# Moving row scatters off the products' ends, one block's scores ahead of the fourth turn, and the first tile's transposes into the fifth turn

## The chip, the cores and the metric

The kernel runs on one core of a Trainium2 chip. The metric is the time of one execution on the device in microseconds (us). The core has five engines with queues of their own: PE (TensorE, matrix products and transposes), DVE (VectorE), ACT (ScalarE), POOL (GpSimd) and SP (SyncE, which here issues DMAs). PSUM is the memory that PE writes its results to; SBUF holds everything else on the chip.

## The reference

Two steps: a linear attention with decay over 4 batches, 8 heads and 768 positions, worked through block by block with a running state, and a mixture of experts that sends each of the 3072 resulting rows (512 values) to one of 8 experts.

```
# attention, for each block of rows (the reference uses 64, the kernel 128)
intra = (qb @ kb.T) * Dmask;  intra = intra @ vb
inter = (qb * lam_pow) @ kv_state
out[:, :, sl] = intra + inter
kv_state = lam_block * kv_state + (kb * rev_pow).T @ vb

# experts, x = the attention's rows
logits = x @ w_gate + modality_bias[modality_id]
e_idx = argmax(logits);  gate_w = probability of that expert
h = maximum(x[mask] @ w1[e], 0)
out[mask] = gate_w[mask] * (h @ w2[e])
```

## The kernel before

**The attention** goes over 24 blocks of 128 rows, numbered 0 to 23, six to a batch. A loop over m (lines 926 to 991) takes the pair a = 2m, b = 2m+1. For each block PE makes the scores (`scores`, L261, tile `s` in two PSUM buffers), DVE multiplies them by the decay mask (`mask`, L267, tile `pt`), ACT scales the keys (`keys`, L243, tile `kd`) and POOL the queries (`query`, L228, tile `qd`); then PE multiplies the queries by the state (`from_state`, L309), the masked scores by the values (`values`, L319), and the keys by the values (`products`, L275, tile `kv`), and DVE adds these products to the state (`add`, L283 and L286). Scores, masks, keys and queries are made one pair ahead. Results gather in the tile `o`, which has two buffers, and are copied to `xt` (`give`, L298), the last block's on DVE.

**Turns.** After each second pair, four blocks (a group, 0 to 5) are turned from columns to rows: `turns(grp, amid)` calls `turn` for two blocks (PE transposes L338, copied on DVE L345 and ACT L348 to the tile `grp`), then `gates` (PE, L356), and then `turn` for two more. The last group comes later, within the first products of the experts. The third group stands in m = 5, the fourth in m = 7, the fifth in m = 9.

**Routing.** For each third of the rows (8 blocks) DVE chooses experts and slots. The many small DVE instructions are a list from which `do(n)` takes the next n (they show up as L384). Then eight scatters (`one_slot`, L439) write rows to `placed`, a tensor in the chip's main memory, in the order of their experts: a short POOL copy (L442) and an indirect DMA that POOL issues (L443). They wait in the list `jobs`, and `tick(mm)` takes the next one and ties its DMA to a PE instruction `mm`. The eight scatters of the first third are called 0 to 7 here; they enter the list after the third group's turn in m = 5, and all must be issued by m = 8, where `need("slots")` empties the list and the first tile of rows is fetched.

**The first tile of the experts.** `fetch_x(0)` (L616, SP) reads 512 rows back from `placed` into `xg` with four DMAs; it waits for the landing of the last scatter. `turn_rows(0)` transposes them on DVE in two halves (L690), `split_rows` makes a rounded part and a rest of them (ACT and DVE, tile `xhl`), and `low_w1` and `split` make the rest `low` of the weights (DVE, L915 and L611). All of that feeds the first layer (L702 to L704), of which PE does a first part ahead of the last group's turn. From there on PE works through the experts' tiles.

**The order.** PE, DVE, ACT and SP run their instructions in the order in which the code issues them. POOL's are chained in theirs by `pool()`. Nothing is reordered by a scheduler; a tick adds a wait and does not place anything on PE.

Of the kernel before, what the change touches and what calls it, by code (L numbers as in the profile page):

```python
# [15 lines left out]
P = 128  # L16
# [27 lines left out]
def linear_attention_moe(tc, qkv, lam, modality, wg, mbias, w1, w2, out):  # L44
    nc = tc.nc
    with ExitStack() as ctx:
# [199 lines left out]
        scs = {}  # L246
# [9 lines left out]
        def scores(g):  # L256
            kt, qt, vt, kn = loaded(g)
            scs[g] = ps.tile([P, 2, NP, P], F32, name="s", bufs=2)
            for p in range(NP):
                for hl, r in enumerate(halves2):  # L260
                    mm = nc.tensor.matmul(scs[g][:, hl, p, :], kt[r, p, :], qt[r, p, :], start=True, stop=True)  # L261
            begun[g] = mm
            return mm
# [93 lines left out]
                                          start=(p == 0), stop=(p == NP - 1), tile_position=(0, t * Q))  # L357
            return mm

        def turns(grp, amid):  # L360
            turn(grp, 0)
            turn(grp, 1)
            mm = gates(grp)
            do(4)
            amid()
            turn(grp, 2)
            return mm, turn(grp, 3)

        shape = [P, RC, E]

# [317 lines left out]
        def turned(out, rows):  # L688

            return nc.vector.transpose(out=out.rearrange("q p (t a) -> q t p a", a=Q),  # L690
                                       in_=rows.rearrange("q t (p a) -> q t p a", a=Q))

        def turn_rows(n):
            for h in range(2):
                turned(xt2[:, :, h * P : (h + 1) * P], xgs[n][:, 4 * h : 4 * (h + 1), :])

        def split_rows():
            for i in range(2):
# [126 lines left out]
        xgs = {}  # L825
# [30 lines left out]

        pairs = B * NC // HB
        def block(g, on_pool=False):
            mm = scores(g)
            mask(g)  # L860
            keys(g, on_pool)
            query(g)
            return mm
# [62 lines left out]
        for m in range(2, pairs):  # L926
            a, b = HB * m, HB * m + 1
            ahead = m + 1 < pairs
            add(b)
            if m == 4 or m == 8:  # L930
                routed = m // 4 - 1, *choose(m // 4 - 1, gate_rows())
            if ahead:
                block(a + 2)
                mm = block(b + 2)
                if m > 4:
                    tick(mm)
                if 2 < m <= pairs - SLOTS:
                    after(load(m + SLOTS - 1, [1]), mm)
                if m == 9:
                    fetch_w1(*some, parts=range(2, 4))  # L940
                elif m == 10:
                    fetch_w2(*some, parts=range(2, 4))
            if m == 5 or m == 9:
                ranks(routed[-1])
                slots += slots_of(*routed)
            if m == 10:
                w1h = w1_part("w1h", F32R, True)
                w1l0 = [work.tile([P, KC, TT], F32R, name="low", tag=f"both{i}" if i < 4 else "dk", bufs=1) for i in range(1, 5)]
                nc.scalar.copy(out=w1h[0], in_=raw1[0])
                do(4)  # L950
                turn_rows(0)
            elif not ahead:
                split_rows()
                low_w1(0)
                split(raw1[1], w1h[1], w1l0[1])
                do(4)
            elif m == 2:
                routing_constants()
            elif m == 3:
                clear(slice(E * CAP, E * CAP + TT), TT)  # L960
            if m < 10:
                do(7 if m % 4 == 0 else 8)
            if m == 2:
                mm = values(b, begins=True)
                from_state((a, b), ends=True)
            elif not ahead:
                values(a, begins=True)
                mm = values(b, begins=True)
                from_state((a, b), ends=True)
            else:  # L970
                from_state((a, b))
                values(a)
                mm = values(b)
            if m == 4 or m == 8:
                do(1)
            if m > 4:
                tick(mm)
            if m + SLOTS < pairs:
                load(m + SLOTS, [0])
            if ahead:  # L980
                mm = products(a + 2)
                mm = products(b + 2) or mm
                if m == 7:
                    tick(mm)
                add(a + 2)
            if m % 2 and ahead:
                ends = turns(m // 2, begin_list)
                if m == 5 or m == 9:
                    jobs += [("slots", one_slot)] * RC
                for mm in ends[: 2 if m % 4 == 1 else 1] if m > 4 else ():  # L990
                    tick(mm)
            if m == 8:
                need("slots")
                raw1 = w1_part("raw1", F32)
                some = fetch_regs(0, True)
                fetch_w1(*some, parts=range(2))
                fetch_x(0)
            elif m == 9:
                raw2 = w2_part("raw2", F32)
                some = fetch_regs(0, True)  # L1000
                fetch_w2(*some, parts=range(2))
                fetch_x(1)
# [195 lines left out]
```

## Time and profile before

| what | us |
|---|---|
| median of 3 runs | 383.61 (383.05 to 384.69) |
| the profiled execution | 384.85 |
| its span | 383.1 |
| PE busy | 373.5 |
| DVE busy | 282.9 |
| ACT busy | 237.4 |
| POOL busy | 99.0 |

The span is what the trace covers, from the first instruction to the last. A timeline gives for each stretch of like instructions its start, its duration from the first start to the last end, the engine and line, the tile written and those read, their shapes and the number of instructions. Idle time of the engine just before it, when there is any that counts, stands at the end in brackets with what ended it. The end of a matrix product in the record is modelled and reaches into the next one's start by about 0.07 us. A POOL row of an indirect DMA is the time that POOL takes to write its descriptors, not the transfer.

### The profile page before, as it was taken

How to read it: one execution, taken by the hardware profiler on the slowest of the kernel's cores; microseconds unless marked ns; L12 is line 12 of the kernel's file. 1: busy time of each engine (PE TensorE's matmuls, PEld its weight loads, DVE VectorE, ACT ScalarE, POOL GpSimd, SP SyncE). 2: the span in 40 equal slices, each digit the busy share in tenths (PEclk: the TensorE clock that was granted, in tenths of full speed). 3: DMA queues.
4: the chain of work that ended last, by engine and by line, in shares of the span. 5: the costliest groups of instructions: out<-in, count | busy, mean ns of one | idle time of the engine just before them, and what ended most of it. 6: DMA issues, size and time to landing. Idle time of an engine off the chain costs nothing.

```text
span 383.1 us, 9168 instructions
## 1 busy us (share of the span) xinstructions
PE 373.5 (97%) x3316; PEld 318.1 (83%) x3316; DVE 282.9 (74%) x506; ACT 237.4 (62%) x458; POOL 99.0 (26%) x130
## 2 busy tenths in 40 slices
PE   8999999999999999999999999999999999999993
PEld 3889989888998889888888877788878888888882
DVE  6677978779777889867789584486876868688630
ACT  1577676777766765564766664456566665776621
POOL 3653238628600177020100102102011020201112
PEclk9999999999999999999999999999999999999998
DMA  7999988999979684599714899763870210300100
GB/s 246 386 408 385 363 315 282 394 294 354 295 255 292 230 232 180 220 347 326 208 52 122 268 409 313 285 191 91 290 233 30 56 55 19 93 0 3 55 29 27
DMA packets 44597, 82.69 MB, mean 216 GB/s; under 512 B 7406, under 2 KB 20222, under 8 KB 44544
## 3 DMA queue, kind: packets, MB, share of 16 engines
q1 hardware_dynamic: 40592, 69.23, 55.6%
q0 software_dynamic: 3952, 12.79, 8.8%
q8 instruction: 28, 0.46, 0.5%
q14 instruction: 25, 0.20, 0.2%
HBM read 89.52 MB, written 17.85 MB: 280 GB/s over the span
## 4 chain that ended last, share of the span: by engine, by line
PE 56%; issue 33%; POOL 5%; DVE 3%; DMA 2%; SPq 0%; POOLq 0%; ACT 0%; DVEq 0%
PE s L742 8%; PE o L702 6%; PE o L704 6%; PE o L703 6%; PE s L261 6%; PE o L319 5%; POOL out_dram L770 4%; PE o L338 3%; PE s L741 3%; PE o L309 3%; PE kv L275 2%; DMA load<-in_qkv_dram 2%; PE x L356 1%; PE s L704 1%; PE kv L702 1%
## 5 line engine op out<-in xcount | busy, mean ns | idle before, releaser
L742 PE MATMUL s<-xhl,w1h 128*128 128x512 f32 x320 | 108.2, 395 | 0.0
L770 POOL DMA_INDIRECT out_dram<-y,idx x24 | 28.7, 1198 | 213.1 <-ACT y L769 167.8
L702 PE MATMUL o<-w2h,hh 128*128 128x512 f32 x192 | 75.1, 391 | 0.0
L703 PE MATMUL o<-w2l,hh 128*128 128x512 f32 x192 | 74.8, 389 | 0.0
L704 PE MATMUL o<-w2h,hl 128*128 128x512 f32 x192 | 74.7, 389 | 0.0
L741 PE MATMUL s<-xhl,w1l 128*128 128x256 f32 x240 | 67.2, 280 | 0.0
L742 PEld LDWEIGHTS s<-xhl,w1h 128*128 128x128 f32 x320 | 55.2, 188 | 7.7 <-issue 0.4
L751 DVE TENSOR_TENSOR hs<-s,hb 128x512 f32<-128x512 f32 x40 | 27.6, 690 | 43.8 <-ACT hb L749 43.8
L611 DVE TENSOR_TENSOR w1l<-raw,w1h 128x1024 fp32r<-128x1024 f32 x44 | 51.7, 1220 | 2.0 <-ACT w1h L610 2.0
L753 DVE TENSOR_TENSOR w2l<-raw,w2h 128x1024 fp32r<-128x1024 f32 x40 | 48.6, 1215 | 0.0
L741 PEld LDWEIGHTS s<-xhl,w1l 128*128 128x128 f32 x240 | 45.1, 188 | 3.6
L610 ACT CAST w1h<-raw 128x1024 fp32r<-128x1024 f32 x47 | 46.0, 1045 | 0.0
L752 ACT ACTIVATE hh<-hs 128x512 fp32r<-128x512 f32 x40 | 25.3, 633 | 30.7 <-DVE hs L751 29.9
L702 PEld LDWEIGHTS o<-w2h,hh 128*128 128x128 f32 x192 | 36.0, 188 | 7.8 <-issue 0.8
L704 PEld LDWEIGHTS o<-w2h,hl 128*128 128x128 f32 x192 | 36.0, 188 | 7.6
L703 PEld LDWEIGHTS o<-w2l,hh 128*128 128x128 f32 x192 | 36.1, 188 | 7.3
L735 ACT CAST w2h<-raw 128x1024 fp32r<-128x1024 f32 x40 | 41.5, 1038 | 0.0
L243 ACT ACTIVATE kd<-load,dk 128x64 f32<-128x64 f32 x144 | 35.7, 336 | 2.4 <-DMA load<-in_qkv_dram 2.3
L610 ACT CAST xhl<-xt 128x512 fp32r<-128x512 f32 x24 | 13.7, 619 | 30.9 <-DVE xt L690 29.7
L443 POOL DMA_INDIRECT placed<-grp,sloti x24 | 26.7, 1114 | 20.5 <-PE o L338 8.2
L228 POOL TENSOR_TENSOR qd<-load,pq 128x512 f32<-128x512 f32 x20 | 25.3, 1280 | 24.5 <-PE s L261 20.2
L267 DVE TENSOR_TENSOR pt<-s,dk 128x1024 f32<-128x1024 f32 x24 | 28.5, 1213 | 3.0 <-PE s L261 2.9
(209 smaller groups left out, 584.9 us busy)
## 6 DMA issues: line engine op xcount, KB each, us to landing
raw<-in_w_dram SPq DMA_DIRECT2D x96, 512.0 KB
load<-in_qkv_dram SPq DMA_DIRECT2D x12, 1024.0 KB
both<-in_w_dram SPq DMA_DIRECT2D x16, 512.0 KB
xg<-placed SPq DMA_DIRECT2D x48, 128.0 KB
placed<-blank SPq DMA_DIRECT2D x9, 528.0 KB
load<-in_qkv_dram SPq DMA_DIRECT2D x8, 512.0 KB
load<-in_qkv_dram SPq DMA_DIRECT2D x2, 2048.0 KB
load<-in_qkv_dram SPq DMA_DIRECT2D x4, 768.0 KB
```

The lines of the kernel that those rows point to most:

```text
L243: nc.scalar.activation(out=kds[g][:, p, hl, :], in_=kn[:, p, hl, :], func=AF.Copy, scale=dk[:, hl, p, P - 1 : P])
L267: nc.vector.tensor_tensor(out=pts[g], in0=scs.pop(g), in1=dk, op=ALU.mult)
L610: nc.scalar.copy(out=hi, in_=src)
L611: nc.vector.tensor_tensor(out=lo, in0=src, in1=hi.bitcast(F32), op=ALU.subtract)
L702: nc.tensor.matmul(out, ah, bh, start=first, stop=False)
L703: nc.tensor.matmul(out, ah, bl, start=False, stop=False)
L704: return nc.tensor.matmul(out, al, bh, start=False, stop=last)
L735: nc.scalar.copy(out=w2h[i], in_=raw2[i])
L741: nc.tensor.matmul(hp[:, j, :TT], w1l[i][:, kc, fs], xh[c][:, d, :], start=False, stop=False)
L742: mm = nc.tensor.matmul(hp[:, j, :], w1h[i][:, kc, fs], xhl[c][:, d].rearrange("p h t -> p (h t)"), start=(kc == 0), stop=(kc == KC - 1))
L753: nc.vector.tensor_tensor(out=w2l[i], in0=raw2[i], in1=w2h[i].bitcast(F32), op=ALU.subtract)
L770: sc = nc.gpsimd.indirect_dma_start(out=out, out_offset=bass.IndirectOffsetOnAxis(ap=idx[:, t, 0:1], axis=0), in_=y, in_offset=None, bound ...
```

## The change

`tick`s are set at other places in m = 6, 7 and 8; in m = 7 the scores of block 18 are issued ahead of the fourth group's turn rather than behind it, and `block(18)` then finds them made; `turn_rows(0)` is cut in two halves, of which one is issued between the first two and the last two copies of the fifth group's turn (m = 9) and one behind them; in m = 10 the addition of block 21 goes behind the two masks; `low_w1(0)` goes from m = 11 to m = 10; and four of the small routing instructions (`geB`, `ntB`, `baseB`) go from m = 10 to m = 11, behind `low`. Nothing is computed that was not computed before, and nothing is left out.

```diff
--- before.py
+++ after.py
@@ -357,14 +357,17 @@
                                           start=(p == 0), stop=(p == NP - 1), tile_position=(0, t * Q))
             return mm
 
-        def turns(grp, amid):
+        def turns(grp, amid, rows=lambda h: None):
             turn(grp, 0)
             turn(grp, 1)
             mm = gates(grp)
             do(4)
             amid()
+            rows(0)
             turn(grp, 2)
-            return mm, turn(grp, 3)
+            last = turn(grp, 3)
+            rows(1)
+            return mm, last
 
         shape = [P, RC, E]
 
@@ -690,9 +693,12 @@
             return nc.vector.transpose(out=out.rearrange("q p (t a) -> q t p a", a=Q),
                                        in_=rows.rearrange("q t (p a) -> q t p a", a=Q))
 
+        def turn_half(n, h):
+            turned(xt2[:, :, h * P : (h + 1) * P], xgs[n][:, 4 * h : 4 * (h + 1), :])
+
         def turn_rows(n):
             for h in range(2):
-                turned(xt2[:, :, h * P : (h + 1) * P], xgs[n][:, 4 * h : 4 * (h + 1), :])
+                turn_half(n, h)
 
         def split_rows():
             for i in range(2):
@@ -856,7 +862,7 @@
 
         pairs = B * NC // HB
         def block(g, on_pool=False):
-            mm = scores(g)
+            mm = None if g in scs else scores(g)
             mask(g)
             keys(g, on_pool)
             query(g)
@@ -926,13 +932,18 @@
         for m in range(2, pairs):
             a, b = HB * m, HB * m + 1
             ahead = m + 1 < pairs
-            add(b)
+            if m != 10:
+                add(b)
             if m == 4 or m == 8:
                 routed = m // 4 - 1, *choose(m // 4 - 1, gate_rows())
             if ahead:
+                if m == 7:
+                    tick(scores(a + 2))
                 block(a + 2)
                 mm = block(b + 2)
-                if m > 4:
+                if m == 10:
+                    add(b)
+                if m == 5 or m > 7:
                     tick(mm)
                 if 2 < m <= pairs - SLOTS:
                     after(load(m + SLOTS - 1, [1]), mm)
@@ -947,13 +958,11 @@
                 w1h = w1_part("w1h", F32R, True)
                 w1l0 = [work.tile([P, KC, TT], F32R, name="low", tag=f"both{i}" if i < 4 else "dk", bufs=1) for i in range(1, 5)]
                 nc.scalar.copy(out=w1h[0], in_=raw1[0])
-                do(4)
-                turn_rows(0)
+                low_w1(0)
             elif not ahead:
                 split_rows()
-                low_w1(0)
                 split(raw1[1], w1h[1], w1l0[1])
-                do(4)
+                do(8)
             elif m == 2:
                 routing_constants()
             elif m == 3:
@@ -973,21 +982,23 @@
                 mm = values(b)
             if m == 4 or m == 8:
                 do(1)
-            if m > 4:
+            if m == 5 or m > 7:
                 tick(mm)
             if m + SLOTS < pairs:
                 load(m + SLOTS, [0])
             if ahead:
                 mm = products(a + 2)
                 mm = products(b + 2) or mm
-                if m == 7:
+                if m == 6 or m == 7:
                     tick(mm)
                 add(a + 2)
+                if m == 7:
+                    scores(a + 4)
             if m % 2 and ahead:
-                ends = turns(m // 2, begin_list)
+                ends = turns(m // 2, begin_list, (lambda h: turn_half(0, h)) if m == 9 else lambda h: None)
                 if m == 5 or m == 9:
                     jobs += [("slots", one_slot)] * RC
-                for mm in ends[: 2 if m % 4 == 1 else 1] if m > 4 else ():
+                for mm in ends if m > 4 else ():
                     tick(mm)
             if m == 8:
                 need("slots")
```

PE in m = 7 and 8, before: values of blocks 14 and 15 (L319), products of block 16 (L275), the fourth group's turn with its gates (L338, L356), and the scores of 18 and 19 (L261).

```order
L319 MATMUL o<-pt,load 64x128 x16
L275 MATMUL kv<-load,kd 64x64 x8
L338 MATMUL o<-ident,xt 128x128 x8
L356 MATMUL x<-xt,wgq 32x128 x16
L338 MATMUL o<-ident,xt 128x128 x8
L261 MATMUL s<-load 128x128 x16
L309 MATMUL o<-qd,state_126 64x128 x2
```

After:

```order
L319 MATMUL o<-pt,load 64x128 x16
L275 MATMUL kv<-load,kd 64x64 x8
L261 MATMUL s<-load 128x128 x8
L338 MATMUL o<-ident,xt 128x128 x8
L356 MATMUL x<-xt,wgq 32x128 x16
L338 MATMUL o<-ident,xt 128x128 x8
L261 MATMUL s<-load 128x128 x8
L309 MATMUL o<-qd,state_126 64x128 x2
```

The eight score products of block 18 now stand ahead of the first transposes; those of block 19 stay.

POOL from scatter 5 on, before (`qd_1340` is the query of block 19, the next two those of 20 and 21; block 18 begins a batch and has none):

```order
L442 COPY grp_415<-pay_112 128x16
L443 DMA placed_117<-grp_415,sloti_895 26880x528
L442 COPY grp_415<-pay_112 128x16
L443 DMA placed_117<-grp_415,sloti_895 26880x528
L442 COPY grp_415<-pay_112 128x16
L443 DMA placed_117<-grp_415,sloti_895 26880x528
L228 TENSOR_TENSOR qd_1340<-load_943,pq_99 128x512
L228 TENSOR_TENSOR qd_1457<-load_1118,pq_99 128x512
L228 TENSOR_TENSOR qd_1479<-load_1118,pq_99 128x512
```

After:

```order
L445 COPY grp_415<-pay_112 128x16
L446 DMA placed_117<-grp_415,sloti_895 26880x528
L445 COPY grp_415<-pay_112 128x16
L446 DMA placed_117<-grp_415,sloti_895 26880x528
L228 TENSOR_TENSOR qd_1338<-load_943,pq_99 128x512
L445 COPY grp_415<-pay_112 128x16
L446 DMA placed_117<-grp_415,sloti_895 26880x528
L228 TENSOR_TENSOR qd_1457<-load_1114,pq_99 128x512
L228 TENSOR_TENSOR qd_1479<-load_1114,pq_99 128x512
```

Scatters 5 and 6 still stand ahead of the query of block 19, scatter 7 now behind it; the places of scatters 2 to 4 in the row are the same as before. What the scatters wait for is in the ticks. Scatter 2: the end of the products of block 15 (before: the scores of block 15). Scatter 3: the scores of block 16 (before: the values of block 13). Scatter 4: the products of block 16 (before: the scores of block 17). Scatter 5: the fourth group's gates (before: the values of block 15). Scatter 6: the last transpose of the fourth group (before: the products of block 16). Scatter 7: the scores of block 19 (before: the fourth group's gates).

DVE from the first copies of the fifth group's turn on, before (`sloti` is the slots of the second third; `state` the additions of blocks 20, 21 and 22):

```order
L345 COPY grp<-o 64x512 x2
L384 TENSOR_TENSOR sloti<-slot,m8s 128x8
L345 COPY grp<-o 64x512 x2
L286 SCALAR_TENSOR_TENSOR state_126<-state_125,pq,kv 128x64 x4
L267 TENSOR_TENSOR pt<-s,dk 128x1024 x2
L384 TENSOR_TENSOR geB<-x,thr 128x104
L384 TENSOR_REDUCE ntB<-geB 128x8
L384 MEMSET baseB 128x1
L384 TENSOR_TENSOR baseB<-ebase,nA 128x8
L690 STREAM_TRANSPOSE xt_132<-xg 128x4x4x32 x2
L286 SCALAR_TENSOR_TENSOR state_127<-state_126,pq,kv 128x64 x4
L611 TENSOR_TENSOR xhl_133<-xt_132,xhl_133 128x2x256
```

After:

```order
L345 COPY grp<-o 64x512 x2
L387 TENSOR_TENSOR sloti<-slot,m8s 128x8
L693 STREAM_TRANSPOSE xt_132<-xg 128x4x4x32
L345 COPY grp<-o 64x512 x2
L693 STREAM_TRANSPOSE xt_132<-xg 128x4x4x32
L267 TENSOR_TENSOR pt<-s,dk 128x1024 x2
L286 SCALAR_TENSOR_TENSOR state_126<-state_125,pq,kv 128x64 x4
L921 TENSOR_TENSOR low<-raw_1405,w1h 128x1024
L286 SCALAR_TENSOR_TENSOR state_127<-state_126,pq,kv 128x64 x4
L614 TENSOR_TENSOR xhl_133<-xt_132,xhl_133 128x2x256
L614 TENSOR_TENSOR xhl_134<-xt_132,xhl_134 128x2x256
L614 TENSOR_TENSOR low<-raw_1405,w1h 128x1024
```

The two transposes of `xg` now stand on either side of the last two copies, ahead of the masks; an addition has changed places with the masks; `low` stands ahead of the second addition, and `geB` and the rest have left the stretch. Behind the last row shown the second half of `xhl`, the second `low`, `geB`, `ntB`, `baseB`, four more small ones and the copy of the last `xt` follow. Between the two copies rows of before and the copy of the last `xt`, both orders hold the same instructions.

## Rows read from the trace of the kernel before

**Rows 1.** The page, part 1: busy time, share of the span, instructions.
```profile
PE 373.5 (97%) x3316; PEld 318.1 (83%) x3316; DVE 282.9 (74%) x506; ACT 237.4 (62%) x458; POOL 99.0 (26%) x130
```

**Rows 2.** Timeline of PE, 63 to 99 us: start, duration, line, tiles, count, [idle, releaser].
```profile
63.29 1.65 PE L309 MATMUL o<-qd,state 64*64 64x128 f32 x32
...
66.67 0.63 PE L275 MATMUL kv<-load,kd 128*64 128x64 f32 x16
...
69.91 1.23 PE L338 MATMUL o<-ident,xt 128*128 128x128 f32 x8 [0.27 <-DVE grp L345]
...
71.07 2.06 PE L261 MATMUL s<-load 64*128 64x128 f32 x32
...
73.06 1.10 PE L309 MATMUL o<-qd,state 64*64 64x128 f32 x32
...
82.04 1.10 PE L275 MATMUL kv<-load,kd 128*64 128x64 f32 x32
...
86.15 2.06 PE L261 MATMUL s<-load 64*128 64x128 f32 x32
...
94.54 0.28 PE L703 MATMUL s<-xhl,w1h 128*128 128x256 f32 x1
...
96.05 0.38 PE L704 MATMUL s<-xhl,low 128*128 128x256 f32 x1 [1.23 <-DVE low L915]
...
98.76 0.49 PE L338 MATMUL o<-ident,xt 128*128 128x128 f32 x3
```

**Rows 3.** Timeline of DVE, three additions to the state, same columns.
```profile
62.45 1.62 DVE L286 SCALAR_TENSOR_TENSOR state<-state,pq,kv 128x64 f32<-128x64 f32 x8 [0.90 <-PE kv L275]
...
68.32 0.86 DVE L286 SCALAR_TENSOR_TENSOR state<-state,pq,kv 128x64 f32<-128x64 f32 x4 [1.08 <-PE o L338]
...
83.22 0.85 DVE L286 SCALAR_TENSOR_TENSOR state<-state,pq,kv 128x64 f32<-128x64 f32 x4 [1.17 <-PE kv L275]
```

**Rows 4.** Timeline of POOL, four of the scatters and a query product.
```profile
57.01 0.98 POOL L443 DMA_INDIRECT placed<-grp,sloti  x1 [0.28 <-POOL grp L442]
...
60.98 1.03 POOL L443 DMA_INDIRECT placed<-grp,sloti  x1 [0.28 <-PE kv L275]
...
66.95 1.03 POOL L443 DMA_INDIRECT placed<-grp,sloti  x1 [0.28 <-PE kv L275]
...
71.92 0.99 POOL L443 DMA_INDIRECT placed<-grp,sloti  x1 [0.52 <-issue]
...
89.12 2.52 POOL L228 TENSOR_TENSOR qd<-load,pq 128x512 f32<-128x512 f32 x2
```

**Rows 5.** Timeline of DVE, 85 to 99 us.
```profile
85.82 1.28 DVE L345 COPY grp<-o 64x512 f32<-64x512 f32 x2 [0.48 <-PE o L338]
...
97.56 0.67 DVE L298 COPY xt<-o 128x512 f32<-128x512 f32 x1
```

**Rows 6.** Chain of waits, two pieces in order of time: start, us, what.
```profile
90.52 0.08 DVE baseB L384
90.61 0.98 issue
```

**Rows 7.** Timeline of SP's issues: row fetches of the first tile and a later one.
```profile
78.09 2.36 SPq L629 DMA_DIRECT2D xg<-placed  x4
...
203.36 1.88 SPq L629 DMA_DIRECT2D xg<-placed  x4
```

**Rows 8.** Transfers of the scatters' queue, 60 to 61 and 77 to 78 us.
```profile
q0 software_dynamic: 1, 0.00, 0.0%
...
q0 software_dynamic: 5, 0.01, 3.2%
```

**Rows 9.** Packets by size, 84 to 85, 85 to 86 and 207 to 208 us.
```profile
DMA packets 219, 0.21 MB, mean 208 GB/s; under 512 B 109, under 2 KB 177, under 8 KB 219
...
DMA packets 111, 0.33 MB, mean 334 GB/s; under 512 B 26, under 2 KB 30, under 8 KB 111
...
DMA packets 87, 0.02 MB, mean 21 GB/s; under 512 B 79, under 2 KB 86, under 8 KB 86
```

## The prediction

> **What bounds the kernel now.** I read the page first: PE is busy for 373.5 of 383.1 us [rows 1], so only PE's own waits can be won, and only those on its way to the experts' products, which follow each other without a hole. Next PE's timeline through the stretch that the diff touches, and there one looks for a stage that lasts longer than the same stage elsewhere. There are three such places [rows 2].
>
> (a) The state products of blocks 14 and 15 last 1.65 us where those of 18 and 19 last 1.10: 0.55 lost. The reason stands in DVE's timeline: the addition that they need began at 62.45 after 0.90 us of idleness [rows 3], behind a scatter that POOL wrote from 60.98 to 62.01 [rows 4].
>
> (b) From the products of block 16 to the scores of 18, 66.67 to 71.07, it takes 4.40 us. The same stretch in the fifth group, 82.04 to 86.15, takes 4.11 with twice the products (1.10 where the fourth has 0.63), so 3.64 without them: about 0.8 lost, 0.27 of it shown as waiting for the `grp` copies. The addition of block 16, whose products ended at 67.30, began at 68.32, just after the scatter of 66.95 to 67.98 [rows 2 to 4]. Where no scatter runs, after the products that ended at 83.14, the addition began at 83.22 [rows 2, 3]. So a scatter over the products' end holds the addition by about 1 us, twice.
>
> (c) The first product with `low` waits until 96.05; its neighbour began at 94.54. These small products follow each other within some 0.12 us (0.28 overlapped), so 1.39 us is lost, 1.23 of it named as waiting for DVE's `low` [rows 2]. DVE has no gap from 85.82 to 98.23 (97.56 + 0.67) [rows 5], and the chain of waits runs there too [rows 6]: `low` is late because of its own work, 12.41 us of it.
>
> What can be won in all is 0.55 + 0.8 + 1.39 = 2.75 us. The last group's turn, at 98.76, ends the stretch [rows 2]; what this row gains or loses the whole kernel does, since PE doesn't stop behind it.
>
> **The change part by part.**
>
> Scatters 2 and 4 now wait for the end of the products with which the additions start, where they used to run over that end. Addition and scatter are released by the same PE instruction; POOL needs about 0.28 us more after a release [rows 4], DVE 0.08 [rows 3], so the addition is under way first. I take the whole of (a), 0.55. If the scatter held the addition nonetheless, nothing is won here; a loss is excluded as far as the addition goes, since it waits a full scatter already.
>
> The scores of block 18 ahead of the fourth turn give the `xt` copy and the additions a further 1.0 us of PE's time (half of the 2.06 [rows 2]) as cover; the tile they write has been free since the masks of the pair before. I take all of (b), 0.8; if the `grp` copies stay late, 0.27 stays. Sum so far: PE reaches the scores of block 20 some 1.35 us earlier (0 to 1.4).
>
> Scatter 7 pays for that. It was issued at 71.92 [rows 4], waiting for the gates. Now it stands behind scatter 6, which waits for the last transpose, and behind the query of block 19. The last transpose ends where the scores of block 19 start: 71.07 + 1.0 - 1.35 = 70.7. Scatter 6 then starts at about 71.2 (0.5 behind its releaser, as the 0.52 of scatter 7 [rows 4]) and takes 1.0; the query takes 1.26 (half of 2.52 [rows 4]), with its own wait 0.5; the copy 0.2, and again 0.3 to 0.5: about 74.5 (74.0 to 75.4), 2.6 us later than before.
>
> The fetch of the first tile's rows waits for that scatter's landing. It was issued at 78.09 [rows 7], 6.17 after scatter 7, with the scatters' queue still moving its last 5 packets in 77 to 78 [rows 8]. It landed so slowly beside the first weights, whose DMAs SP issues just ahead of the fetch. A scatter in a quieter time, of 57.01, had at 60 to 61 a last packet [rows 4, 8]: 3 to 4 us, say 3.6. So the fetch goes out at 74.5 + 3.6 to 75.4 + 6.2, 78.1 to 81.6. I take 80.7, with the 6.17, since the same weights are on their way.
>
> The rows land after that. Before, the packets of row size (under 2 KB less those under 512 B) were 68 in 84 to 85 and 4 in 85 to 86 [rows 9]: 7 to 7.9 us after the issue. A later fetch without other traffic, of 203.36, had 7 left in 207 to 208 [rows 7, 9]: up to 4.6. In the new place the first weights have mostly gone through while the second part's come behind it, so I take a little above the quiet one, 5.0, and so a landing L of 85.7 (82.7 to 89.5).
>
> Ahead of the last two `grp` copies, where the first transpose goes, DVE was free from 85.34 on (85.82 less 0.48 of idleness [rows 5]). What it does before that is released by PE, so it comes there at 85.34 - 1.35, about 84.0. So in the middle case it waits there for 1.7 us, and what is queued behind are the last two `grp` copies, for whose tiles PE waits with the next state products, then the masks, the additions, `xhl`, `low` and the copy of the last `xt`, without which the last group cannot be turned.
>
> From the first transpose to the end of that copy DVE has the same instructions as before from 85.82 to 98.23 in another order, 12.41 us. One of them was long: `baseB` started at 90.52, and 0.98 us from 90.61 on the chain waits for nothing that the profile shows [rows 6], while POOL's query product ran from 89.12 to 91.64 [rows 4]. In its new place no query runs, so I count 12.41 - 0.98 = 11.43 (ends: 11.43 and 12.41, if the stall has another cause).
>
> The two parts of `low` and the additions in other places add nothing: they are within these 11.43. PE's own way to the last turn is shorter in this case: with the copies done at L + 1.9 = 87.6, and from the state products to the turn 98.76 - 88.13 - 1.39 = 9.24 (88.13 is 86.15 and the 1.98 of the scores, as from 71.07 to 73.06), it is there at 96.9.
>
> **The sum.** The last turn starts at L + 11.55 (twice 0.06 from a release to a start, on DVE and on PE) = 85.7 + 11.55 = 97.25, against 98.76: 1.5 us gained. Another 0.1 goes to waits like the 0.27 of [rows 2], of which the new order will have some: I forecast 1.4. The profiled run took 384.85, its span 383.1, with 1.75 around it; the change doesn't touch that. The median of the runs shown is 383.61, 1.24 below the profiled one, and I carry the gain over as it is: 383.6 - 1.4 = 382.2.
>
> **The rivals.**
>
> B, the rows come in time. If scatter 7 lands as the quiet one did, the fetch goes out at about 78.1 and the rows are there at 82.7, before DVE is. Nothing waits then, and all of 2.75 is won: 380.9. For it speaks that it starts 2.6 us later, when the first weights are further on; against it, that it took 6.17 before, and that those weights stay ahead of the fetch. Between B and the forecast the time goes with L, one for one. A page speaks for B: the Trainium skill, "DMA: Bandwidth & Descriptors", section "Anatomy of one DMA — SWDGE (gpsimd) path", fits a transfer that POOL issues with 2.0 us and bytes over 436e3, by which a scatter of 128 rows of 2112 bytes would land, as an estimate, 2.6 us after the issue; the 6.17 in this trace disagrees. Chance of B: 0.27.
>
> C, the rows come late. If scatter 7 goes out at 75.4, lands 6.2 later and the fetch needs the 7.9 that it needed before, L is 89.5, the turn starts at 101.05, and the time is 383.6 + 2.3 = 385.9. It decides from L = 87.2 on; above it the kernel is slower than before. For it speaks that the fetch stood among the weights before, and that the second part of the weights is issued right behind it; against it, that the first part has had 2.6 more us to pass. Chance: 0.08.
>
> D, the scatters still hold the additions, now from the products' end on. Then (a) and (b) stay lost, and PE wins only (c): 1.39, about the forecast's time, 382.2 to 382.5, through another cause; DVE would come to the first transpose at 85.3, and wait 0.4 for it. Chance: 0.1.
>
> The forecast's own chance is 0.55, with 381.6 to 383.4.
>
> **How the numbers follow.** A measurement of this kernel tells about 0.5% from no change, 1.9 us. Faster than that, below 381.7, needs L under 85.3 or so: most of B, and the lower edge of the forecast, 0.32 together. Slower by that, above 385.5, is only the end of C: 0.06. The rest, 0.62, is within 0.5%. The range goes from B's 380.9 to what L = 88 would give, 384.4.
>
> **What would show it.** In the profile of the changed kernel: the state products of 14 and 15 last 1.1, and the additions start 0.1 behind the products (else D); the fourth turn has no wait; scatter 7 goes out near 74.5 and the fetch near 80.7 (near 78 would be B); on DVE the first transpose stands alone with a wait of about 1.6 us for the fetched rows; `baseB` takes 0.15; `low` has no wait on PE. It would be wrong if the fetch took less than 4 us or more than 6.5, or if PE found another late partner, such as the keys on ACT, whose order is unchanged while PE comes earlier.

## The result, and the profile of the changed kernel

The changed kernel takes 387.7 us in the median of six runs (386.09 to 388.76), the kernel before 383.62 (383.05 to 384.69): the ratio is 1.0103, with a 95% interval from 1.0077 to 1.0128. It is 1% slower, 4.1 us, where 1.4 us less was forecast. The profiled execution took 388.76 us, its span is 387.1.

PE's timeline of the changed kernel (start, duration, line, tiles, count, idle time before and its releaser), to be set against [rows 2]:

```profile
63.29 1.10 PE L309 MATMUL o<-qd,state 64*64 64x128 f32 x32
...
85.19 2.06 PE L261 MATMUL s<-load 64*128 64x128 f32 x32
90.96 2.57 PE L309 MATMUL o<-qd,state 64*64 64x128 f32 x32 [3.72 <-DVE grp L345]
93.46 3.54 PE L319 MATMUL o<-pt,load 128*64 128x128 f32 x32
96.83 0.63 PE L275 MATMUL kv<-load,kd 128*64 128x64 f32 x16
...
103.11 1.04 PE L338 MATMUL o<-ident,xt 128*128 128x128 f32 x8
```

The state products of 14 and 15 take 1.10 us and not 1.65, PE is at the scores of 22 and 23 at 85.19 and not at 86.15, and the wait for `low` is gone. Then comes a hole that was not there: the state products of 20 and 21 start at 90.96, after 3.72 us in which PE waited for the `grp` copies, and they and the values behind them take 2.57 and 3.54 us, where 1.10 and 1.97 are usual. The last group's turn starts at 103.11, in [rows 2] at 98.76. DVE shows what the copies waited for:

```profile
89.53 0.71 DVE L693 STREAM_TRANSPOSE xt<-xg 128x512 f32<-128x512 f32 x1 [5.16 <-DMA xg<-placed]
...
97.54 0.86 DVE L286 SCALAR_TENSOR_TENSOR state<-state,pq,kv 128x64 f32<-128x64 f32 x4 [1.39 <-PE kv L275]
```

The first transpose of the fetched rows, now ahead of the last two copies, waited 5.16 us for the fetch. The second addition of this list waited again, 1.39 us, for the products of 22, which PE made late. The chain of waits leads back from the transpose, pieces in order of time, start, us, what:

```profile
75.41 7.63 DMA placed<-grp,sloti
...
83.06 0.34 SPq L632
...
86.28 3.13 DMA xg<-placed
```

Scatter 7 was issued at 75.41, its landing took 7.63 us, the fetch of the rows went out at 83.06 at once, and the last of its four DMAs, issued late at 86.28, landed 3.13 us later. Just ahead of the scatter, SP had issued the first weights, 1 MB in two DMAs:

```profile
75.14 0.93 SPq L684 DMA_DIRECT2D raw<-in_w_dram  x2
```

PE's clock stands in the view of windows (window, us, PE busy and instructions, granted clock, DMA share, GB/s):

```profile
85.00:88.00 3.00, 2.24 (x35) 1.00 0.54 163
...
92.00:93.00 1.00, 1.00 (x25) 0.50 1.05 415
...
97.00:98.00 1.00, 1.00 (x30) 1.00 1.15 233
```

The granted clock is 1.00 (2.4 GHz) until the hole, 0.50 (1.2 GHz) behind it, and 1.00 again in the window from 97 us on. What PE did before it fell is clear: nothing, since 87.2.

### The profile page after: what moved, and what is told of

Same layout as the page of the kernel before. It is cut to its first block, busy times and chain, and to the rows that moved or that the text cites. A ratio compares the mean times of both kernels' runs of the same rounds, so it can differ in the third digit from the quotient of the medians.

```text
span 387.1 us, 9168 instructions
## 1 busy us (share of the span) xinstructions
PE 375.6 (97%) x3316; PEld 320.7 (83%) x3316; DVE 283.9 (73%) x506; ACT 237.1 (61%) x458; POOL 99.5 (26%) x130
## 4 chain that ended last, share of the span: by engine, by line
PE 55%; issue 33%; POOL 5%; DMA 4%; SPq 1%; DVE 1%; ACT 0%; POOLq 0%; DVEq 0%
PE s L748 8%; PE o L708 6%; PE o L709 6%; PE o L710 6%; PE o L319 5%; PE s L261 5%; POOL out_dram L776 4%; PE o L309 3%; PE s L747 3%; PE o L338 2%; PE kv L275 2%; DMA placed<-grp,sloti 2%; DMA load<-in_qkv_dram 2%; PE x L356 1%; PE kv L708 1%
## 5 line engine op out<-in xcount | busy, mean ns | idle before, releaser
L708 PE MATMUL o<-w2h,hh 128*128 128x512 f32 x192 | 75.1, 391 | 0.0
```

Source lines behind the costliest of these rows:

```text
L708: nc.tensor.matmul(out, ah, bh, start=first, stop=False)
```

## Where the time went

A second profile of the kernel before is the better measure, since it took 383.14 us, as most executions do (the first took 384.85). Its PE timeline:

```profile
63.27 1.10 PE L309 MATMUL o<-qd,state 64*64 64x128 f32 x32
...
66.10 0.64 PE L275 MATMUL kv<-load,kd 128*64 128x64 f32 x16
...
70.02 2.06 PE L261 MATMUL s<-load 64*128 64x128 f32 x32
...
85.10 2.06 PE L261 MATMUL s<-load 64*128 64x128 f32 x32
87.08 1.10 PE L309 MATMUL o<-qd,state 64*64 64x128 f32 x32
...
89.92 0.63 PE L275 MATMUL kv<-load,kd 128*64 128x64 f32 x16
...
95.00 0.39 PE L704 MATMUL s<-xhl,low 128*128 128x256 f32 x1 [1.23 <-DVE low L915]
...
97.70 1.03 PE L338 MATMUL o<-ident,xt 128*128 128x128 f32 x8
```

From it to the changed kernel the turn of the last group goes from 97.70 to 103.11, 5.4 us, in these pieces:

| piece | before, second profile | changed | difference |
|---|---|---|---|
| PE at the scores of 22 and 23 | 85.10 | 85.19 | +0.1 |
| from there to the state products | 1.98 | 5.77 | +3.8 |
| from there to the products of 22 | 2.84 | 5.87 | +3.0 |
| from there to the last turn | 7.78 | 6.28 | -1.5 |

The third line is work at half the clock, the last is the wait for `low` that went. Executions of the changed kernel differ in the pieces. In a second profile, of 387.3 us, they are +0.7, +2.2, +2.2 and -1.5, and DVE's wait is 3.57 us instead of 5.16:

```profile
88.56 0.71 DVE L693 STREAM_TRANSPOSE xt<-xg 128x512 f32<-128x512 f32 x1 [3.57 <-DMA xg<-placed]
```

PE's values behind it, in part at the lower clock, take 2.85 us, and the turn comes at 101.30:

```profile
92.35 2.85 PE L319 MATMUL o<-pt,load 128*64 128x128 f32 x32
...
101.30 1.04 PE L338 MATMUL o<-ident,xt 128*128 128x128 f32 x8
```

## The experiments

Theory M: the transposes stand ahead of copies that PE needs, and the rows that they read come 5 us after DVE asks for them. Its rivals: T, the later scatters cost the time wherever the rows are used; R, the new place of the transposes is bad whatever the scatters do.

**The transposes back behind the masks.** The ticks and all else stay as changed.

```diff
-                ends = turns(m // 2, begin_list, (lambda h: turn_half(0, h)) if m == 9 else lambda h: None)
+                ends = turns(m // 2, begin_list)
...
+                turn_rows(0)
                 low_w1(0)
```

> The changed kernel with only the two transposes of the fetched rows put back behind the masks of m = 10 (ticks, scores of block 18, addition, low and the small list stay changed). Theory M (the transposes stand ahead of copies that PE needs, and the rows come 5 us after DVE asks for them): the fetch still goes out near 83 us and lands near 89.5, but DVE now asks for the rows only at about 89.8, after copies, masks and addition, so it waits for nothing; PE has no wait at the state products of 20 and 21, its clock stays at full, and the last group's turn starts at about 97.1 against 98.8 in the kernel before: some 1.6 us faster than before, about 382.0. Rival T (the later scatters themselves cost the time, since the rows come 5 us later wherever they are used): still 2 us or more slower than before.

Measured: 383.0 us, ratio 0.9982 (0.9966 to 0.9999). PE and then DVE:

```profile
96.83 1.06 PE L338 MATMUL o<-ident,xt 128*128 128x128 f32 x8 [0.44 <-DVE xt L298]
```

```profile
89.53 1.30 DVE L693 STREAM_TRANSPOSE xt<-xg 128x512 f32<-128x512 f32 x2
```

The fetch went out at 83.93, even later than in the changed kernel, and nobody waited: DVE comes to the transposes without a wait, and PE's state products keep their place and clock. Between the two medians, 387.7 and 383.0, lies nothing but the place of these two instructions: M stands and T falls. The turn came at 96.83, near the 97.1 expected, but the time fell by 0.5 us and not 1.6. Part of the 1.6 was never there: it was reckoned from the turn at 98.76 in the first profile, and against the usual 97.70 the turn gains 0.9. The rest is lost behind the turn: the last products start 277.28 us after it, where the kernel before needs 276.44 (below).

**The ticks of before, the transposes in the new place.**

```diff
-                if m == 7:
-                    tick(scores(a + 2))
...
-                if m == 5 or m > 7:
+                if m > 4:
                     tick(mm)
...
-                if m == 6 or m == 7:
+                if m == 7:
                     tick(mm)
...
-                for mm in ends if m > 4 else ():
+                for mm in ends[: 2 if m % 4 == 1 else 1] if m > 4 else ():
```

> The changed kernel with the six ticks of the kernel before (transposes in the fifth turn, scores of 18 ahead of the fourth turn, addition, low and list as changed). Theory M: scatter 7 goes out near 72 again, the fetch near 78, the rows land at 85 to 86; DVE waits for them 0.5 to 1.5 us instead of 5.2, PE stays busy enough to keep its clock, and the last turn starts near 97.3: 1 to 1.5 us faster than before, about 382.3. Rival R (the place of the transposes is bad by itself, whatever the scatters do): a wait of 3 us or more stays on DVE, and the time is over 385.

Measured: 383.8 us, 0.9994 (0.9977 to 1.0012). DVE's first transpose:

```profile
86.14 0.71 DVE L693 STREAM_TRANSPOSE xt<-xg 128x512 f32<-128x512 f32 x1 [1.81 <-DMA xg<-placed]
```

The wait is 1.81 us, a little over the expected bound, and PE's clock stays at 1.00. R as it was put, a wait of 3 us or more and a time over 385, falls too. But the 382.3 expected did not come either, and the turn, put near 97.3, came at 98.18: even with the old ticks the new place costs something, since DVE waits in it (with the old place and one further edit, worth 0.6 us, the turn is at 96.24, below). Lateness without the place cost DVE no wait in the run before. The rows come at 86.0, only 3.4 us earlier than in the changed kernel, though scatter 7 went out 4.1 us earlier, at 71.32: the fetch itself now takes 8.8 us, from 77.21 to 86.02, beside the weights.

**Only the ticks and the scores of block 18**, DVE's order of m = 9 to 11 as before (the diff of the change without its lines on `rows`, `add(b)`, `low_w1`, `do(8)`).

> The kernel before with only the ticks and the scores of block 18 changed (DVE's order in m = 9 to 11 as before). Theory M: PE is 1 us ahead at the scores of block 20 as in the changed kernel, the fetch is as late as there (83, landing 89.5), yet DVE asks for the rows only at about 90.6, so nothing waits for them; the wait for low stays as it was: 0.9 us faster than before, about 382.7. Rival T: the late rows cost here too, 2 us or more slower than before.

Measured: 383.59 us, 0.9996 (0.9980 to 1.0013): nothing gained. T falls here a second time, but so does the 0.9 us that was expected. The second profile of the kernel before, run next, says why.

**The kernel before, once more.**

> The kernel before once more, unchanged, for a second profile. The first profile (384.85 us, last group's turn at 98.76) lay 1.2 us above the median of its runs. Theory S (the three losses that the prediction added up, 2.75 us, are usually smaller than in that one profile): the turn starts near 98.0 here, with less than 2.75 of waits in the three places, and the time is near 383.5. Rival (the losses are there in every execution and the excess lies elsewhere): 98.7 or later for the turn, the three places as in the first profile.

Measured: 383.14 us, with the turn at 97.70: theory S, as far as (a) and (b) go. In its PE timeline above the state products of 14 and 15 take 1.10 us: loss (a) is not there. From the products of 16 to the scores of 18 it takes 3.92, not 4.40 [rows 2]: of (b) 0.28 is left. Loss (c) is there, 1.23 of waiting. The scatter that was blamed for (a) lies where it lay, POOL first and DVE then:

```profile
60.95 1.02 POOL L443 DMA_INDIRECT placed<-grp,sloti  x1 [0.28 <-PE kv L275]
```

```profile
61.35 0.17 DVE L384 TENSOR_REDUCE atA<-pastA 128x2 f32<-128x16 f32 x1
61.44 1.62 DVE L286 SCALAR_TENSOR_TENSOR state<-state,pq,kv 128x64 f32<-128x64 f32 x8
```

It runs from 60.95 to 61.97 over the products' end at 61.36, as in [rows 4], and the addition starts at 61.44 all the same, right behind the instruction before it, not at 62.45 [rows 3]. So a scatter over a products' end does not hold the addition by 1 us as a rule; it did so twice in one execution. Of 30 runs of the kernel before taken with the first four experiments two were over 384.6 us, so the first profile was one of the rare ones. What makes the difference between two executions in which scatter and products lie alike was not found.

**PE kept busy through the wait.**

```diff
-            for p in range(NP):
-                for hl, r in enumerate(halves2):
+            for _ in range(3 if g >= 22 else 1):
+                for p in range(NP):
+                    for hl, r in enumerate(halves2):
...
```

> The changed kernel with the scores of blocks 22 and 23 computed three times over instead of once (same values into the same tiles; four blocks of score products more, some 4.1 us of PE work, in the place where PE stood idle for 3.8 us). Theory I (the granted clock of PE fell to half because PE stood idle): the state products of 20 and 21 take 1.1 us instead of 2.6 and the values 2.0 instead of 3.5, and although the kernel does more work it is about 2.8 us faster than the changed one: 384.9. Rival (the clock fell for another reason, such as the transfers at that time): both stay slow, and the time is 387.7 or more.

Measured: 387.28 us, 1.0083 (1.0059 to 1.0108) against the kernel before. PE and DVE:

```profile
85.29 5.63 PE L262 MATMUL s<-load 64*128 64x128 f32 x96
...
91.70 1.09 PE L310 MATMUL o<-qd,state 64*64 64x128 f32 x28 [0.16 <-DVE grp L346]
92.72 1.97 PE L320 MATMUL o<-pt,load 128*64 128x128 f32 x32
95.31 0.69 PE L276 MATMUL kv<-load,kd 128*64 128x64 f32 x16 [0.62 <-DVE state L287]
...
101.67 1.04 PE L339 MATMUL o<-ident,xt 128*128 128x128 f32 x8
```

```profile
89.68 0.71 DVE L694 STREAM_TRANSPOSE xt<-xg 128x512 f32<-128x512 f32 x1 [5.20 <-DMA xg<-placed]
```

DVE waited as long as in the changed kernel and the transfers were the same, but PE never stood idle, and its state products and values take 1.09 and 1.97 us: the clock fell because PE idled. The time expected was wrong, though: 0.4 us below the changed kernel's median instead of 2.8, and the turn 1.4 us below the first profile's. PE at full speed waits for DVE instead: its state products stand behind the `grp` copies to 91.70, and the products of 22 wait 0.62 us for the addition. They start at 95.31, against 96.83 in the changed kernel, so of the 3.0 us at half the clock 1.5 come through to them. From there PE has no named wait up to the turn, and DVE's copy of the last `xt` ended at 101.13 (100.46 + 0.67), 0.5 us before it.

**The fetch ahead of the weights on SP.**

```diff
-                fetch_w1(*some, parts=range(2))
                 fetch_x(0)
+                fetch_w1(*some, parts=range(2))
```

> The changed kernel with SP's two steps in m = 8 exchanged: the fetch of the first tile's rows is issued ahead of the first two weight DMAs, so that neither scatter 7 nor the fetch has that 1 MB beside it. Theory W (the scatter's landing takes 7.6 us and the fetch 6.4 because the weights are on the same DMA engines): scatter 7, issued at 75.4, lands within 4.5 us, the fetch goes out near 79.5 and the rows land near 84.5, DVE waits 0.5 us or less, PE keeps its clock and the last turn starts near 96.5: 382.3. Rival (the landing is slow by itself, or other transfers slow it as much): fetch at 82 or later, a wait of 3 us or more, 386 or more.

Measured: 383.78 us, 0.9993 (0.9978 to 1.0009). SP, DVE, PE, and a piece of the chain:

```profile
79.48 1.96 SPq L632 DMA_DIRECT2D xg<-placed  x4
```

```profile
84.41 0.71 DVE L693 STREAM_TRANSPOSE xt<-xg 128x512 f32<-128x512 f32 x1
```

```profile
96.63 1.06 PE L338 MATMUL o<-ident,xt 128*128 128x128 f32 x8
...
103.07 0.66 PE L338 MATMUL o<-ident,xt 128*128 128x128 f32 x4 [0.60 <-ACT grp L348]
```

```profile
86.78 11.27 DMA raw<-in_w_dram
```

Theory W holds for the rows: scatter 7, issued at 75.40, was answered by the fetch at 79.48, 4.1 us instead of 7.6, DVE took the rows at 84.41 without waiting, and the turn started at 96.63, within 0.2 of what was expected; the time, put at 382.3, was not. The Trainium skill, "DMA: Bandwidth & Descriptors", section "Anatomy of one DMA — SWDGE (gpsimd) path", would give 2.6 us for this scatter, as an estimate; even without the weights beside it the measured time is longer, and with them three times as long. But the weights are now late in turn: a DMA for the second layer's, issued at 86.78, took 11.27 us, and ACT's cast of them waited 4.01 us. PE waits 0.60 us behind the turn for copies that stand on ACT behind these casts, and 0.33 later on. The last products start 278.75 us after the turn, 276.44 in the kernel before: what was won was given back, though of these 2.3 us only 0.93 are named as PE's waits.

**Scatter 7 ahead of the query of block 19.**

```diff
                 for mm in ends if m > 4 else ():
                     tick(mm)
+                if m == 7:
+                    tick(mm)
```

> The changed kernel with scatter 7 tied to the last transpose of the fourth turn like scatter 6, so that it stands right behind that one and ahead of the query of block 19 (one place in POOL's order, 1.2 us earlier; the query is 1.7 us later, 3 us before PE needs it). Theory W: at 74.2 it is issued ahead of the weights of 75.1 and lands in about 5 us, the fetch goes out near 79 and, among the weights, the rows land near 86.5; DVE waits 2.3 us, the turn starts near 98.0: 383.6. Rival (a plain delay, no matter what it runs beside): everything 1.2 us earlier than in the changed kernel, rows at 88.3, turn near 101: 386.

Measured: 383.72 us, 1.0008 (0.9999 to 1.0018). The time is as expected, but not in the way expected. POOL and DVE:

```profile
74.08 0.98 POOL L446 DMA_INDIRECT placed<-grp,sloti  x1 [0.52 <-POOL grp L445]
75.09 1.29 POOL L228 TENSOR_TENSOR qd<-load,pq 128x512 f32<-128x512 f32 x1
```

```profile
74.72 1.75 DVE L387 TENSOR_TENSOR eq<-l,mx 128x64 f32<-128x64 f32 x1
...
77.16 1.32 DVE L387 TENSOR_TENSOR l<-l,mx 128x64 f32<-128x64 f32 x1
...
85.97 0.71 DVE L693 STREAM_TRANSPOSE xt<-xg 128x512 f32<-128x512 f32 x1 [0.34 <-DMA xg<-placed]
```

Scatter 7 went out at 74.08, and the fetch at 80.78: 6.7 us, not 5, so being ahead of the weights of 75.1 helps it by 0.9 us only. The rows are there at 85.9, and DVE waits 0.34 us, because DVE itself is late: two small instructions that take 0.22 us elsewhere take 1.75 and 1.32. The queries of POOL, now later, run from 75.09 to 76.38 and from 77.13 on, just over them; this is what was read from `baseB` [rows 6], which took 0.16 us in its new place in the changed kernel. The Trainium skill, "SBUF — State Buffer", section "Who interferes with whom", says that a VectorE instruction with two SBUF inputs contends with a GpSimd one that reads SBUF, and that the order of issue decides which one is blocked. The trace agrees with the contention, 1.75 and 1.32 us against 0.22; on the order it does not bear out the page, since by the recorded starts `eq`, at 74.72, was 0.37 us ahead of the query and was held all the same.

**The copy of the last `xt` ahead of the small list**, on top of the transposes back behind the masks.

```diff
                 split(raw1[1], w1h[1], w1l0[1])
-                do(8)
...
                 from_state((a, b), ends=True)
+                do(8)
```

> The changed kernel with the transposes back behind the masks (as in the run with that edit alone) and the eight small list instructions of m = 11 behind the copy of the last xt rather than ahead of it. In the run with the first edit alone PE waited 0.44 us for that copy at the last turn, which started at 96.83. Theory M: the turn starts at 96.4, and the time is 0.4 us below that run, 382.6. Rival (the turn's start no longer sets the time, since the later weights now do): 383.0, as that run.

Measured: 383.28 us, 1.0004 (0.9993 to 1.0016), from 382.44 to 385.06. The turn came at 96.21, as expected, and the last products at 373.54:

```profile
96.21 1.04 PE L338 MATMUL o<-ident,xt 128*128 128x128 f32 x8
...
373.54 1.96 PE L819 MATMUL o<-both,hnt 128*32 128x128 f32 x64
```

That is 277.33 us later, 0.9 more than in the kernel before (97.70 to 374.14). Neither side of the expectation gives the whole picture: the profiled execution was 0.7 us faster than the profile of the run without this edit, and the median 0.3 slower. Why its executions spread as they do was not found.

**The same with the ticks of before.**

> As the run with the transposes back and the copy first, but with the six ticks of the kernel before (kept of the change: the scores of block 18, the addition behind the masks, low in m = 10, the small list in m = 11, there behind the copy). Theory V (the new ticks make the first fetch, and through SP's order the later weights, 5 us later, which took back 0.9 us between the last turn and the last product): the fetch goes out near 77, the turn starts at 96.2 as there, the last products follow after 276.5 us instead of 277.3, and the time is near 381.8, ratio 0.9955. Rival (what was lost after the turn has nothing to do with the fetch): 382.7, no better than with the new ticks.

Measured: 382.14 us, 0.9971 (0.9962 to 0.9980). PE, to be set beside the last fence:

```profile
96.24 1.04 PE L338 MATMUL o<-ident,xt 128*128 128x128 f32 x8
...
372.71 1.96 PE L819 MATMUL o<-both,hnt 128*32 128x128 f32 x64
```

The turn starts as early, and the last products follow after 276.47 us: V holds. The way from the ticks there can be read on SP, the first fetch and the first part of the second layer's weights, and on ACT, the first cast of these weights. With the new ticks:

```profile
82.74 2.36 SPq L632 DMA_DIRECT2D xg<-placed  x4
...
88.83 1.34 SPq L688 DMA_DIRECT2D raw<-in_w_dram  x2
```

```profile
96.40 1.05 ACT L613 CAST w2h<-raw 128x1024 fp32r<-128x1024 f32 x1 [2.43 <-DMA raw<-in_w_dram]
```

With the old ones:

```profile
77.17 2.36 SPq L632 DMA_DIRECT2D xg<-placed  x4
...
83.93 0.87 SPq L688 DMA_DIRECT2D raw<-in_w_dram  x2
```

```profile
93.89 1.06 ACT L613 CAST w2h<-raw 128x1024 fp32r<-128x1024 f32 x1
```

SP issues in order, so a fetch that goes out 5.6 us later puts these weights 4.9 us later, and the cast, which finds them there with the old ticks, waits 2.43 us for them. From there on ACT and DVE run 0.9 us later (DVE's `low` that PE needs next starts at 104.11 and not 103.21, and PE loses 0.4 us there), and the last products start 0.87 later after a turn at the same time. So the new ticks cost 0.9 us between these two profiles, and 1.1 between the medians, in a kernel in which DVE does not wait for the rows themselves. They cost nothing behind the turn in the run with only the ticks changed: there the fetch went out as late, at 83.85, the cast waited 2.12 us, and the last products still came 276.44 us after the turn; that turn, at 97.88, is 1.7 us later than here.

**And without the scores of block 18 ahead.**

```diff
                 add(a + 2)
-                if m == 7:
-                    scores(a + 4)
```

> The same without the scores of block 18 ahead of the fourth turn: the kernel before with DVE's order in m = 10 and 11 alone changed. In the second profile of the kernel before PE was at the scores of block 20 at 75.87, as early as every kernel with the scores ahead. Theory S (that step has nothing to win in a usual execution): the same time as the run above within 0.2 us, 381.8. Rival (the step wins the 0.3 us that stand between the products of 16 and the scores of 18): 0.3 us slower than the run above.

Measured: 382.08 us, 0.9970 (0.9958 to 0.9982), 0.06 us from the run with them: theory S. PE:

```profile
75.81 2.06 PE L261 MATMUL s<-load 64*128 64x128 f32 x32
```

It is at the scores of block 20 at 75.81, not later than with that step. This is the kernel before with DVE's order in m = 10 and 11 changed and nothing else: the masks ahead of one addition, `low` sooner, the small list behind the last copy. Set against runs of the kernel before of the same time, it is 1.3 us faster; the changed one was 4.1 slower.

**The changed kernel, once more.** Its rows stand under the second section.

> The changed kernel once more, unchanged, for a second profile (the first was the slowest of its six runs, 388.76 us; the median was 387.7). Theory M: the same picture, with DVE's wait for the rows 4 to 5.5 us and PE at half its clock after its idle time for 3 to 6 us; wherever this execution is shorter, it is by a shorter half-clock stretch or an earlier landing, one for one. Rival (the wait was an accident of one profile, as two of the losses of the kernel before were): a wait of under 2 us, and a time near 384.

387.3 us: the wait of 3.57 us is shorter than expected, but the picture is the same, and the rival falls. The kernel before, run once beside it, took 385.07, more than its usual time.

## The prediction, step by step

Two steps failed: the losses that were to be won, and the landing L of the fetched rows. The first took most of the gain away, the second made the kernel slower. What should follow from a late landing was seen rightly in kind, in rival C.

**The losses (a) and (b)** were read rightly from one profile and taken for the kernel's. This is the first step that failed. That profile lay 1.24 us above the median, which the prediction noted, and then "I carry the gain over as it is". The excess was mostly the gain: (a) is 0 and (b) 0.28 in the second profile, whose turn is at 97.70 and not 98.76, and all new ticks and scores together are worth nothing (0.9996). Only (c), which hung on DVE's own chain, was there in all three profiles with DVE's old order, and the run without ticks, scores and new transposes gains 1.3 us by it, for the 1.39 forecast.

**The landing L** is the step that turned the sign. It was put at 85.7, and the rows landed at 89.41, so that DVE waited 5.16 us where 1.7 was put. The miss of 3.7 us has three parts. Scatter 7 was put at 74.5 and came at 75.41, 0.9 later: the sum started scatter 6 from the last transpose and left out scatter 5 ahead of it, tied to the gates; POOL takes 1.7 us for each. Its landing was put at 6.17, as before, "since the same weights are on their way", and took 7.65, 1.5 more. The fetch was put at 5.0, as if the first weights had mostly passed, and took 6.35, 1.35 more. The weights had not passed: SP issues 1 MB of them at 75.14, 0.3 us ahead of the scatter, where in the kernel before the scatter, at 71.92 [rows 4], was 4.35 us ahead of them:

```profile
76.27 0.93 SPq L681 DMA_DIRECT2D raw<-in_w_dram  x2
```

Without them beside it the scatter landed in 4.1 us and the fetch in 4.7, so they are the largest part of the last two misses; the late scatter itself comes from POOL's order.

**Rival C** described the case, with rows at 89.5, and was given a chance of 0.08, since a late scatter, a slow landing and a slow fetch were counted as three accidents; the last two have the weights as a common cause. That its 89.5 is met so well is partly luck: the landing was 1.4 us longer than its 6.2, the fetch 1.5 shorter than its 7.9. It put the time at 385.9, and 387.7 was measured. Of these 1.8 us about 1.1 is the turn that it counted from, 98.76 instead of 97.70.

**From the rows to the turn** 11.55 us were put, the time of DVE's list with the turn right behind it. In the run that kept PE busy the list took 11.45, for 11.43 forecast, `baseB` at 0.16 included; the expected stall had the right cause. In the changed kernel it took 12.99, of which 1.39 was the second addition waiting for the products of 22, late behind two stages at 1.2 GHz. That PE's own way is shorter did not hold: in both runs the turn came 0.5 us and more behind DVE's copy, at the end of PE's own work.

**The clock** was in no rival. With PE idle for 3.7 us, what followed ran at 1.2 GHz. By the run that kept PE busy this cost the turn 1.4 us in the first profile, and 0.4 us between the medians.

**The signs** that it named: the state products of 14 and 15 take 1.1 us and the first addition starts 0.07 behind its products, as forecast. The second starts 1.1 behind them, at 67.88; no scatter stands there now, but a small DVE instruction (`atA`) that takes 2.01 us under POOL's queries, and PE does not wait for it. `low` has no wait on PE, as forecast.

**After the turn** nothing was expected to change, and in the changed kernel nothing did: 276.44 us to the last products, as before. In the kernels with the transposes put back, whose turn is 1.0 to 1.7 us earlier than in the run with only the ticks changed, the fetch that is late on SP makes later weights late, 0.8 to 0.9 us.

## What to carry to other kernels

Before waits of one profile are added up, set its time against the median: what a profile has above the median may be just the waits that one means to remove, and a second profile costs one run. An instruction that waits for a transfer belongs behind everything in its queue that another engine needs, unless the transfer is sure to be early; here two transposes of 0.7 us each, waiting for rows, held PE for 3.7 us, and its clock for longer. When a DMA is made later, look at what else its queue issues behind it, and at what its transfer will run beside.

## What the runs showed of the hardware

- The addition that waited 1 us under a scatter in one execution started in 0.08 us in another, with the scatter at the same place to 0.03 us.
- After 3.72 us of idle time PE was granted 1.2 GHz for 6.8 us, nearly to the end of the values of 20 and 21; after 2.12 us in the second profile, for 3.4 us. Kept busy with repeated scores through the same time, beside the same transfers, it stayed at 2.4 GHz.
- A scatter of 128 rows took, from its issue to the start of the fetch that waits for it, 4.1 us with no weights issued until then; 5.6 to 6.2 in five runs with 1 MB of weights issued 3.8 to 4.4 us behind it; 6.7 with them 1.0 us behind it; and 7.2 to 8.6 in six runs with them 0.3 us ahead of it.
